# Decode attention with all of its matmuls in four column tiles, and V as the moving operand

## The chip, the core and the metric

The kernel runs on one core of a Trainium2 chip. The metric is the time of one execution in device microseconds; three runs of the kernel before gave a median of 1196.09 us (1195.54 to 1197.15). Beside them stands one profiled execution, from which all rows of the profile come.

## The reference

Two transformer layers of one decode step, for 8 sequences (batch) with one new token each. Attention and the dense block use the same weights and the same caches in both layers.

```python
# B=8, D=512, Hq=32 query heads, Hkv=8 key heads, Sk=8192 positions, Dh=128, F=1792; all bfloat16
def _A_ref(x, k_cache, v_cache, wq, wo):
    q = (x @ wq)                                  # 32 heads of 128; 4 query heads share a key head
    scores = einsum("bhqd,bhkd->bhqk", q, k) * Dh ** -0.5
    p = softmax(scores)
    o = einsum("bhqk,bhkd->bhqd", p, v)
    return o @ wo
def _B_ref(x, w1, w2):
    return silu(x @ w1) @ w2
x = x + A(layernorm(x)); x = x + B(layernorm(x))
x = x + A(layernorm(x)); x = x + B(layernorm(x))
```

For each of 8 x 8 pairs of sequence and key head, 8192 x 128 keys and as many values (2 MB each) are read and used for 4 query heads, in each of the two layers.

## The kernel before

**Tasks and loads.** A task is one layer, sequence and key head: 128 tasks. `make_tasks` orders them, so that the second layer of one sequence runs beside the first layer of later ones. A task's K comes in four granules of 512 KB, its V in four more; a granule has 16 chunks of 128 positions. The granules land in an arena of 27 slots (`NSLOT`). For 5 of the 8 key heads (20 of 32 granules of K, `KEEP`) K stays in its slots from layer 1 to layer 2, so that 40 of the 128 tasks load V alone. `plan_loads` sorts all 864 loads by the step at which they are needed and gives each a slot; `issue` (L357 to L365) writes them to SP's DMA queue, and `issue_until` sends a load as soon as the program has passed the step at which its slot's last reader stands. SP waits there (L91) for that reader's semaphore. The weights (`wq`, `wo`, `w1`, `w2`) come on the same queue near the start, and stay in SBUF.

**K's layout.** A K load puts 16 consecutive positions (4 KB) into each of 128 partitions; partition p holds positions 64 p + 16 k + c for granule k. A V load reads 512 KB that lie together: partition p holds 16 consecutive positions too, 2048 k + 16 p + c.

```python
src = cache[d.b, d.g].rearrange("(p k c) d -> k p (c d)", k=NGRAN, p=128)[d.k]   # K, L360
```

**The loop.** One loop runs over steps p of half a granule, 8 to a task. In it the instructions of all engines are written out, each engine in this order:

- `emit_q` (L463, L466): PE multiplies `pick`, a matrix of ones and zeros 128 wide, with the task's 4 query columns, four products of 128x4; DVE spreads the result into `QB`.
- `emit_t` (L444): DVE transposes K's granule in place in 32x32 blocks of 32-bit words, 1236 ns each.
- `emit_s` (L481): scores. 16 products a granule, each with 32 columns of `QB` as weights and 128 columns of K moving, in four column tiles (`t`) that write 32 partitions each of `SCp`; four tiles, four partial sums (`n`).
- softmax: `softmax_max` (L491, L493) takes each row's maximum and spreads it; `softmax_shift` (L501) adds it over partitions with an fp32 product with `ones` (128x128), DVE makes the shift (L504, L507); `softmax_exp` (L511) is the exponential on ACT, 128x512, written in permuted order into `P`; `softmax_sum` (L518, L521) adds the sums on DVE and POOL.
- `emit_pt` (L530, L534): PE transposes `P` in four products of 128x128, DVE copies them to `PT`.
- `emit_pv` (L554), `LP` = 14 steps after the scores: for each of 64 chunks, V's chunk (128x128) is the weight and 4 probability columns, each repeated `PVN` = 12 times, move past it; all 64 add up in one tile of `OTp`, 128 partitions by 48.
- `emit_norm` (L568): DVE takes every twelfth column, times the reciprocal sum (L541), as the task's output.
- between them pieces of a chain: the output projection `wo` (L652), the dense block and the next queries (L634), in products of 128x32.

A helper (`op`, `mm_group`) gives every group one semaphore; an engine runs its instructions in the order written, and waits for the readers and writers of the tiles that it touches.

Of the kernel before, what the change touches and what calls it, by code (L numbers as in the profile page):

```python
# [6 lines left out]
DH = 128  # L7
SM_SCALE = DH ** -0.5
# [4 lines left out]
GRP = 8  # L13
# [14 lines left out]
KB = 512  # L28
QUAD = 32
FAR = 1e38  # L30
PVN = 12
CW = 32
SETTLE = 2

# [174 lines left out]
def _build(ctx, nc, A_x, A_k_cache, A_v_cache, A_wq, A_wo, B_w1, B_w2, out):  # L209
# [28 lines left out]
    def sb(shape, dt, name):  # L238
        _cnt[0] += 1
        return ctx.enter_context(nc.sbuf_tensor(f"{name}_{_cnt[0]}", shape, dt))  # L240
# [30 lines left out]
    assert NGRAN == NQ and NPART * QUAD == DH  # L271
    QB = [sb([128, NPART, QUAD], BF16, "QB") for _ in range(NQB)]
    own_q = sb([128, NQ], FP32, "own_q")
    pick = sb([128, NPART, 128], BF16, "pick")
    at1 = [sb([128, HQ], BF16, "at1") for _ in range(3)]
    at2 = QT1[:, :].rearrange("p (b h) -> p h b", h=HQ)
    vr = sb([128, B], FP32, "vr")
# [10 lines left out]
    P = sb([128, KB], BF16, "P")  # L288
    Xr = P
    PT = [sb([128, CPB, NQ * USED], BF16, "PT") for _ in range(NPT)]  # L290
    ones = sb([128, 128], FP32, "ones")
    hm = sb([128, REP], FP32, "hm")
    real = sb([128, 1], FP32, "real")
    far = sb([128, NQ * USED], FP32, "far")
# [30 lines left out]
    def op(eng, inst_fn, reads=(), writes=()):  # L325
        reads = [res(n) if isinstance(n, str) else n for n in reads]
        writes = [res(n) if isinstance(n, str) else n for n in writes]
        syn.acquire(eng, reads, writes)
        inst = inst_fn()
        tok = syn.mark(inst, eng)  # L330
        syn.release(tok, reads, writes)
        return tok
# [10 lines left out]
    def mm_group(steps, reads=(), writes=()):  # L343
        def run():
            inst = None
            for f in steps:
                inst = f()
            return inst
        return op(pe, run, reads, writes)
# [7 lines left out]
    def issue(d):  # L357
        cache = A_k_cache if d.kind == "K" else A_v_cache
        if d.kind == "K":
            src = cache[d.b, d.g].rearrange("(p k c) d -> k p (c d)", k=NGRAN, p=128)[d.k]  # L360
        else:
            src = cache[d.b, d.g].rearrange("(k p c) d -> k p (c d)", k=NGRAN, p=128)[d.k]
        dst = ARENA[:, d.slot * SLOT:(d.slot + 1) * SLOT]
        dma(sp, dst, src, slsem[d.slot], writes=[r_half(d.slot, 0), r_half(d.slot, 1)])
        (k_slot if d.kind == "K" else v_slot)[(d.b, d.g, d.k)] = d.slot  # L365

    with nc.Block() as block:

        @block.sync
        def _(sync_eng):  # L370
# [12 lines left out]
            for n in range(NQB):  # L383
# [9 lines left out]
            op(dve, lambda: dve.tensor_reduce(  # L393
                own_q[:, :], ident[:, :].rearrange("p (c q) -> p c q", q=QUAD), AX.X, ALU.add),
               reads=["ident"], writes=["own_q"])
            for i in range(NPART):
                op(dve, lambda i=i: dve.tensor_copy(
                    pick[:, i, :].rearrange("p (a r) -> p a r", a=NQ),
                    ident[:, i // 2 * 2 * QUAD:(i // 2 + 1) * 2 * QUAD].rearrange("p (r e) -> p e r", e=2)[:, i % 2]
                    .unsqueeze(1).to_broadcast([128, NQ, QUAD])),  # L400
                   reads=["ident"], writes=["pick"])
            for c in range(NQ):
                op(dve, lambda c=c: dve.tensor_scalar(
                    far[:, c * USED:(c + 1) * USED].rearrange("p (r k) -> p r k", k=NGRAN),
# [48 lines left out]
            def emit_q(ti):  # L453
                layer, b, g = tasks[ti]
                if layer == 0:
                    q, rq = QT1[:, b * HQ + g * REP:b * HQ + (g + 1) * REP], f"QT1_{b}"
                else:
                    q, rq = QT2[b % 2][:, g * REP:(g + 1) * REP], f"QT2_{b % 2}"
                n = ti % NQB
                steps = []  # L460
                for i in range(NPART):
                    at = (n * NPART + i) * REP
                    steps.append(lambda i=i, at=at: pe.matmul(  # L463
                        QSp[:, at:at + REP], pick[:, i, :], q, start=True, stop=True))
                mm_group(steps, reads=["pick", rq], writes=[f"QS{n}"])
                op(dve, lambda: dve.tensor_tensor(  # L466
                    QB[n][:, :, 0:USED].rearrange("p i (r a) -> p i r a", a=NQ),
                    QSp[:, n * NPART * REP:(n + 1) * NPART * REP].rearrange("p (i r) -> p i r", r=REP).unsqueeze(3)
                    .to_broadcast([128, NPART, REP, NQ]),
                    own_q[:, :].unsqueeze(1).unsqueeze(1).to_broadcast([128, NPART, REP, NQ]), ALU.mult),  # L470
                   reads=[f"QS{n}", "own_q"], writes=[f"QB{n}"])
# [25 lines left out]

            def softmax_shift(ti):
                ob = ti % 2
                every = OTp[ob][:, 0:NQ * USED]  # L500
                mm_group([lambda: pe.matmul(every, ones[:, :], spread[:, :], start=True, stop=True)],  # L501
                         reads=["ones", "spread"], writes=[f"OT{ob}"])

                op(dve, lambda: dve.scalar_tensor_tensor(  # L504
                    own[:, :], every, real[:, 0:1], far[:, :], op0=ALU.mult, op1=ALU.add),
                   reads=[f"OT{ob}", "real", "far"], writes=["own"])
                op(dve, lambda: dve.tensor_reduce(shift[:, :], own[:, :], AX.X, ALU.min), reads=["own"], writes=["shift"])  # L507

            def softmax_exp(ti):
                bank, st = ti % NSCP, ti % NST  # L510
                op(act, lambda: act.activation(  # L511
                    P[:, :].rearrange("p (x j k) -> p k x j", x=CPB, k=NGRAN),
                    SCp[bank][:, :].rearrange("p (k x j) -> p k x j", k=NGRAN, x=CPB), ACT.Exp, bias=shift[:, 0:1], scale=SM_SCALE, accum_out=rs[st][:, :]),
                   reads=[f"SC{bank}", "shift"], writes=["P", f"rs{st}"])

            def softmax_sum(ti):
# [7 lines left out]
            def emit_pt(ti):  # L524
                pb = ti % NPT
                tb = evacs[0] % NTP
                evacs[0] += 1
                tpv = TPp[tb][:, 0:KB].rearrange("p (c q) -> p c q", q=128)
                steps = [
                    lambda c=c: pe.transpose(tpv[:, c, :], P[:, c * 128:(c + 1) * 128], ident[:, :])  # L530
                    for c in range(CPB)
                ]
                mm_group(steps, reads=["P", "ident"], writes=[f"TP{tb}"])
                op(dve, lambda: dve.tensor_copy(  # L534
                    PT[pb][:, :, :].rearrange("p x (c q) -> p x c q", q=USED),
                    tpv.rearrange("p x (c q) -> p x c q", q=QUAD)[:, :, :, 0:USED]),
                   reads=[f"TP{tb}"], writes=[f"PT{pb}"])
# [5 lines left out]
            def emit_pv(i):  # L543
                ti = i // GPT
                b, g, k, h = where(i)
                slot = v_slot[(b, g, k)]
                ob, pb = ti % 2, ti % NPT
                pv = PT[pb][:, :, :].rearrange("p x (c r k) -> p x c k r", c=NQ, k=NGRAN)
                otp = OTp[ob][:, 0:REP * PVN].rearrange("p (r n) -> p r n", n=PVN)
                steps = []  # L550
                for c in range(GRP):
                    cc = (i % GPT) * GRP + c
                    steps.append(
                        lambda c=c, cc=cc: pe.matmul(  # L554
                            otp, chunk(slot, h * GRP + c), pv[:, cc % CPB, cc // CPB % NQ, k, :].unsqueeze(2).to_broadcast([128, REP, PVN]),
                            start=(cc == 0), stop=(cc == NCH - 1),
                        )
                    )
                mm_group(steps, reads=[r_half(slot, h), f"PT{pb}"], writes=[f"OT{ob}"])

            def emit_norm(ti):
                layer, b, g = tasks[ti]
                ob, st = ti % 2, ti % NST
                if layer == 0:
                    dst, rd = at1[b % 3][:, g * REP:(g + 1) * REP], f"at1_{b % 3}"
                else:
                    dst, rd = at2[:, g * REP:(g + 1) * REP, b], f"QT1_{b}"
                op(dve, lambda: dve.tensor_tensor(dst, OTp[ob][:, 0:REP * PVN:PVN], rcp[st][:, :], ALU.mult),  # L568
                   reads=[f"OT{ob}", f"rcp{st}"], writes=[rd])

            def ln_stages(xv, rx, n):
# [198 lines left out]
            for p in range(NG + LP + GPT + 1):  # L770
# [25 lines left out]
                done = p - LP - GPT  # L796
                if done >= 0 and done % GPT == 0 and done // GPT < ntask:
                    tj = done // GPT
                    emit_norm(tj)
                    layer, b, _g = tasks[tj]  # L800
                    if layer == 0:
                        heads[b].append(_g)
                    elif b == B - 1:
                        heads[B].append(_g)
                    if layer == 0 and tj == last0[b]:
                        assert not chain and turn[0] == b
                        chain.extend([lambda b=b: add_heads(b)] * (HKV - summed[b]) + chain_of(b))
                        chain_b[0] = b
                        turn[0] = b + 1
# [49 lines left out]
```

## Time and profile before

| what | value |
|---|---|
| median of 3 runs | 1196.09 us |
| profiled execution, its own time | 1198.79 us |
| span of its profile | 1197.1 us |
| mean granted PE clock | 0.663 |
| PE / DVE / ACT / POOL busy | 839.0 / 736.1 / 183.5 / 70.8 us |
| share of 16 DMA engines' span taken by packets | 99.1% |
| bytes on SP's queue | 465.12 MB |
| loads of K / of V | 352 / 512, 512 KB each |

The page gives the span in 40 slices, with the busy share of each engine and of the DMA engines in tenths and the rate in GB/s; the queues with their packets; the chain of waits that ended last; and groups of instructions by line, with busy time, mean duration and the idle time before them. "PEld" is the load of weights on PE. A matmul's record includes its latency, so that single records overlap; the time of a group of them is better read from the timeline, which merges them.

### The profile page before, as it was taken

What the parts mean: (1) busy time and instruction counts of PE and PEld (TensorE: products, weight loads), DVE (VectorE), ACT (ScalarE), POOL (GpSimd) and SP (SyncE); (2) the same over time, 40 slices, a digit from 0 to 9 for tenths busy, and PEclk for the clock granted to TensorE, in tenths of its full rate; (3) what the DMA queues carried; (4) which work ended last, traced back from release to release, by engine and by line L of the source; (5) the groups of instructions that cost most, each with busy time, mean ns of one, the idle gap of its engine ahead of it and who ended that gap; (6) DMA issues with size and microseconds to landing.
All of it is one profiled execution on the core that took longest, in us unless ns stands there. A gap on an engine that the chain in (4) does not pass through costs nothing.

```text
span 1197.1 us, 46189 instructions
## 1 busy us (share of the span) xinstructions
PE 839.0 (70%) x20984; PEld 673.4 (56%) x20984; DVE 736.1 (61%) x1830; ACT 183.5 (15%) x266; POOL 70.8 (6%) x172
## 2 busy tenths in 40 slices
PE   1636677767776677767777778777776777677785
PEld 1435566556655566556665566556665656555564
DVE  3736763767456673867457763867376755768464
ACT  0101112111111012111111111111111111111111
POOL 0000000000000000000000000000000000000000
PEclk9955568555765577655866586756775587657765
DMA  9999999999999999999999999999999999999994
GB/s 368 385 396 397 399 355 408 407 394 395 393 408 407 368 389 401 408 404 395 389 408 408 388 397 409 407 402 395 393 407 403 399 393 408 407 392 386 402 408 165
DMA packets 131619, 468.06 MB, mean 391 GB/s; under 512 B 13904, under 2 KB 19808, under 8 KB 130912
## 3 DMA queue, kind: packets, MB, share of 16 engines
q1 hardware_dynamic: 131424, 465.12, 99.1%
q8 instruction: 164, 2.69, 0.9%
q14 instruction: 31, 0.25, 0.1%
HBM read 465.05 MB, written 0.01 MB: 388 GB/s over the span
## 4 chain that ended last, share of the span: by engine, by line
DMA 40%; PE 31%; DVE 15%; issue 9%; SPq 3%; ACT 2%; POOL 0%; POOLq 0%; ACTq 0%; DVEq 0%
DMA arena<-in_A_v_cache_dram 37%; PE OTp L554 14%; PE SCp L481 8%; DVE arena L444 7%; SPq L339 3%; DMA arena<-in_A_k_cache_dram 3%; PE MISC L634 3%; PE OTp L501 2%; PE TPp L530 2%; ACT P L511 2%; DVE rowmax L491 1%; DVE PT L534 1%; PE MISC L652 1%; DVE tr L607 1%; DVE spread L493 1%
## 5 line engine op out<-in xcount | busy, mean ns | idle before, releaser
L554 PE MATMUL OTp<-PT,arena 128*128 128x48 bf16 x8192 | 381.1, 205 | 227.6 <-DMA arena<-in_A_v_cache_dram 182.1
L444 DVE STREAM_TRANSPOSE arena<-arena 128x1024 int32<-128x1024 int32 x352 | 434.9, 1236 | 115.9 <-DMA arena<-in_A_k_cache_dram 115.2
L554 PEld LDWEIGHTS OTp<-PT,arena 128*128 128x128 bf16 x8192 | 316.9, 110 | 331.5 <-DMA arena<-in_A_v_cache_dram 242.6
L511 ACT ACTIVATE P<-SCp,shift 128x512 bf16<-128x512 f32 x128 | 180.3, 1409 | 930.6 <-DVE shift L507 651.5
L481 PE MATMUL SCp<-arena,QB 128*32 128x128 bf16 x8192 | 287.0, 275 | 37.3 <-issue 29.0
L481 PEld LDWEIGHTS SCp<-arena,QB 128*32 128x32 bf16 x8192 | 161.4, 115 | 84.1 <-issue 48.6
L521 POOL PARTITION_ALL_REDUCE ssa<-ssm x128 | 55.6, 435 | 996.0 <-DVE ssm L518 970.8
L534 DVE COPY PT<-TPp 128x256 bf16<-128x256 bf16 x128 | 37.3, 291 | 103.6 <-PE TPp L530 101.8
L501 PE MATMUL OTp<-spread,ones 128*128 128x64 f32 x256 | 75.4, 389 | 25.9 <-DVE spread L493 22.7
L491 DVE TENSOR_REDUCE rowmax<-SCp 128x1 f32<-128x512 f32 x128 | 84.8, 663 | 11.5 <-PE SCp L481 10.3
L530 PE MATMUL TPp<-ident,P 128*128 128x128 bf16 x512 | 68.8, 278 | 13.7 <-ACT P L511 9.6
L504 DVE SCALAR_TENSOR_TENSOR own<-OTp,real,far 128x64 f32<-128x64 f32 x128 | 32.9, 257 | 71.7 <-PE OTp L501 71.7
L501 PEld LDWEIGHTS OTp<-spread,ones 128*128 128x128 f32 x256 | 54.9, 266 | 35.6 <-DVE spread L493 34.4
L518 DVE TENSOR_SCALAR ssm<-hm,rs 128x4 f32<-128x4 f32 x128 | 26.8, 210 | 73.9 <-ACT P L511 73.9
L530 PEld LDWEIGHTS TPp<-ident,P 128*128 128x128 bf16 x512 | 41.7, 122 | 16.5 <-ACT P L511 12.3
L634 PE MATMUL MISC<-xnT,wq 128*128 128x32 bf16 (+1 forms) x1152 | 37.1, 185 | 19.3 <-DVE xnT L621 13.1
L634 PEld LDWEIGHTS MISC<-xnT,wq 128*128 128x128 bf16 x1152 | 35.8, 105 | 20.4 <-issue 16.3
L652 PE MATMUL MISC<-at,wo 128*128 128x32 bf16 x1024 | 37.7, 185 | 6.1 <-issue 4.4
L652 PEld LDWEIGHTS MISC<-at,wo 128*128 128x128 bf16 x1024 | 33.2, 103 | 6.9 <-issue 4.6
L463 PE MATMUL QSp<-QT,pick 128*128 128x4 bf16 x512 | 32.5, 168 | 5.7 <-DVE QT L717 2.9
L493 DVE TENSOR_SCALAR spread<-ident,rowmax 128x64 f32<-128x64 bf16 x128 | 32.6, 255 | 4.5
L511 ACT ACTIVATION_READ_ACCUMULATOR P<-SCp,shift 128x1 f32 x128 | 33.3, 260 | 0.0
(54 smaller groups left out, 276.3 us busy)
## 6 DMA issues: line engine op xcount, KB each, us to landing
arena<-in_A_v_cache_dram SPq DMA_DIRECT2D x512, 512.0 KB, 10.3
arena<-in_A_k_cache_dram SPq DMA_DIRECT2D x352, 512.0 KB, 14.5
wq<-in_A_wq_dram SPq DMA_DIRECT2D x1, 4096.0 KB, 16.6
wo<-in_A_wo_dram SPq DMA_DIRECT2D x1, 4096.0 KB, 26.3
w<-in_B_w_dram SPq DMA_DIRECT2D x2, 1792.0 KB, 22.8
P<-in_A_x_dram SPq DMA_DIRECT2D x1, 8.0 KB
out_dram<-P SPq DMA_DIRECT2D x1, 8.0 KB
```

Of the source, the lines that this page charges most:

```text
L444: op(dve, lambda: dve.transpose(words, words), reads=[r_half(slot, 0), r_half(slot, 1)], writes=[r_half(slot, 0), r_half(slot, 1)])
L481: lambda n=n, t=t: pe.matmul(SCp[bank][t * QUAD:(t + 1) * QUAD, k * 128:(k + 1) * 128], QB[qn][:, n, :], keys[:, t, n // 2, n % 2], start= ...
L491: op(dve, lambda: dve.tensor_reduce(rowmax[:, :], SCp[bank][:, :], AX.X, ALU.max), reads=[f"SC{bank}"], writes=["rowmax"])
L493: op(dve, lambda: dve.tensor_scalar(spread[:, :].rearrange("p (c q) -> p c q", q=USED), lanes, rowmax[:, 0:1], -SM_SCALE, op0=ALU.mult, op ...
L501: mm_group([lambda: pe.matmul(every, ones[:, :], spread[:, :], start=True, stop=True)], reads=["ones", "spread"], writes=[f"OT{ob}"])
L511: op(act, lambda: act.activation(P[:, :].rearrange("p (x j k) -> p k x j", x=CPB, k=NGRAN), SCp[bank][:, :].rearrange("p (k x j) -> p k x ...
L521: op(pool, lambda: pool.partition_all_reduce(ssa[st][:, :], ssm[st][:, :], 128, bass.bass_isa.ReduceOp.add), reads=[f"ssm{st}"], writes=[f ...
L530: lambda c=c: pe.transpose(tpv[:, c, :], P[:, c * 128:(c + 1) * 128], ident[:, :])
L534: op(dve, lambda: dve.tensor_copy(PT[pb][:, :, :].rearrange("p x (c q) -> p x c q", q=USED), tpv.rearrange("p x (c q) -> p x c q", q=QUAD) ...
L554: lambda c=c, cc=cc: pe.matmul(otp, chunk(slot, h * GRP + c), pv[:, cc % CPB, cc // CPB % NQ, k, :].unsqueeze(2).to_broadcast([128, REP, P ...
L634: lambda o=o, k=k: pe.matmul(MISC[:, o * n:o * n + w], w_sb[:, k, o * 128:(o + 1) * 128], rhs_of(k).to_broadcast([128, w]) if n == 1 else ...
L652: lambda o=o, h=h: pe.matmul(MISC[:, o * w:(o + 1) * w], wo_sb[:, h, o * 128:(o + 1) * 128], rhs_of(h).to_broadcast([128, w]) if n == 1 el ...
```

## The change

The change gives every attention product 32 or fewer output partitions, at one of four column tiles.

- **PV**: the 4 probability columns are the weight, and V's chunk moves (128 columns). Chunk `cc` goes to tile `cc % 4`, which writes 4 rows of 128 columns at partition 32 t of `OTp`; so each task ends with four partial sums in four partition groups.
- **fold**, new (`emit_fold`), ahead of `emit_norm`: ACT copies the 128x128 partial sums to SBUF (`OS`), and four fp32 products with `OS` as the weight and a new `pick` (128x4) moving add them up and turn them to 128 partitions by 4.
- **transposes** of `P`: 16 products of 32 columns instead of 4 of 128; exp writes `P` in order.
- **shift**: four fp32 products of 32 columns instead of one of 128.
- **queries**: 16 products with slices of `ident` as weights instead of 4 with `pick`.
- **K's source**: partition 32 a + j now holds positions 2048 a + 512 k + 16 j + c, so that the four partition groups of the scores are four blocks of positions, in the order in which V's granules are used. The runs are 4 KB as before; on the DRAM side the pattern is now 4 blocks x 32 rows x 4 KB, as the program is built, and on the arena's side 128 rows x 4 KB.

```diff
-                src = cache[d.b, d.g].rearrange("(p k c) d -> k p (c d)", k=NGRAN, p=128)[d.k]
+                src = cache[d.b, d.g].rearrange("(a k j c) d -> k a j (c d)", a=NQ, k=NGRAN, j=QUAD)[d.k]
...
-                    steps.append(lambda i=i, at=at: pe.matmul(
-                        QSp[:, at:at + REP], pick[:, i, :], q, start=True, stop=True))
+                    for a in range(NQ):
+                        steps.append(lambda a=a, at=at, pairs=pairs: pe.matmul(
+                            QSp[a * QUAD:(a + 1) * QUAD, at:at + REP], pairs, q, start=True, stop=True))
...
-                every = OTp[ob][:, 0:NQ * USED]
-                mm_group([lambda: pe.matmul(every, ones[:, :], spread[:, :], start=True, stop=True)],
+                every = OTp[ob][:, DH:DH + NQ * USED]
+                mm_group([lambda t=t: pe.matmul(every[t * QUAD:(t + 1) * QUAD, :], ones[:, :], spread[:, :], start=True, stop=True)
+                          for t in range(NQ)],
...
-                    P[:, :].rearrange("p (x j k) -> p k x j", x=CPB, k=NGRAN),
-                    SCp[bank][:, :].rearrange("p (k x j) -> p k x j", k=NGRAN, x=CPB), ACT.Exp, ...
+                    P[:, :], SCp[bank][:, :], ACT.Exp, ...
...
-                    lambda c=c: pe.transpose(tpv[:, c, :], P[:, c * 128:(c + 1) * 128], ident[:, :])
-                    for c in range(CPB)
+                    lambda c=c, k=k: pe.transpose(
+                        tpv[k * QUAD:(k + 1) * QUAD, c, :], P[:, k * 128 + c * QUAD:k * 128 + (c + 1) * QUAD], ident[:, :])
+                    for c in range(CPB) for k in range(NGRAN)
...
-                            otp, chunk(slot, h * GRP + c), pv[:, cc % CPB, cc // CPB % NQ, k, :].unsqueeze(2).to_broadcast([128, REP, PVN]),
-                            start=(cc == 0), stop=(cc == NCH - 1),
+                            OTp[ob][t * QUAD:t * QUAD + REP, 0:DH], pv[:, cc % CPB, cc // CPB % NQ, k, :], chunk(slot, h * GRP + c),
+                            start=(cc < NQ), stop=(cc >= NCH - NQ),
...
+            def emit_fold(ti):
+                ob = ti % 2
+                op(act, lambda: act.copy(OS[:, :], OTp[ob][:, 0:DH]), reads=[f"OT{ob}"], writes=["OS"])
+                folded = OTp[ob][:, DH + NQ * USED:DH + NQ * USED + REP]
+                mm_group([lambda t=t: pe.matmul(folded[t * QUAD:(t + 1) * QUAD, :], OS[:, t * QUAD:(t + 1) * QUAD], pick[:, :],
+                                                start=True, stop=True) for t in range(NQ)],
+                         reads=["OS", "pick"], writes=[f"OT{ob}"])
...
+                    emit_fold(tj)
                     emit_norm(tj)
```

At the start, the four copies that made the old `pick` give way to one reduction for the new one, and `OTp`'s first 128 columns are set to zero.

More of the change, by code (lines that the diff above doesn't have):

```diff
@@ L30 @@
 FAR = 1e38
-PVN = 12
 CW = 32
@@ L273, in _build @@
     own_q = sb([128, NQ], FP32, "own_q")
-    pick = sb([128, NPART, 128], BF16, "pick")
     at1 = [sb([128, HQ], BF16, "at1") for _ in range(3)]
@@ L290, in _build @@
     PT = [sb([128, CPB, NQ * USED], BF16, "PT") for _ in range(NPT)]
-    ones = sb([128, 128], FP32, "ones")
+    ones = sb([128, QUAD], FP32, "ones")
+    pick = sb([128, REP], FP32, "pick")
+    OS = sb([128, DH], FP32, "OS")
     hm = sb([128, REP], FP32, "hm")
@@ L395, in _ @@
                reads=["ident"], writes=["own_q"])
[L396 to L401, printed above, removed]
+            op(dve, lambda: dve.tensor_reduce(
+                pick[:, :], ident[:, :].rearrange("p (c q) -> p q c", q=QUAD)[:, 0:REP, :], AX.X, ALU.add),
+               reads=["ident"], writes=["pick"])
+            for n in range(2):
+                op(dve, lambda n=n: dve.memset(OTp[n][:, 0:DH], 0.0), writes=[f"OT{n}"])
             for c in range(NQ):
@@ L462, in emit_q @@
                     at = (n * NPART + i) * REP
-                    steps.append(lambda i=i, at=at: pe.matmul(
-                        QSp[:, at:at + REP], pick[:, i, :], q, start=True, stop=True))
-                mm_group(steps, reads=["pick", rq], writes=[f"QS{n}"])
+                    pairs = ident[:, i // 2 * 2 * QUAD:(i // 2 + 1) * 2 * QUAD].rearrange("p (r e) -> p e r", e=2)[:, i % 2]
+                    for a in range(NQ):
+                        steps.append(lambda a=a, at=at, pairs=pairs: pe.matmul(
+                            QSp[a * QUAD:(a + 1) * QUAD, at:at + REP], pairs, q, start=True, stop=True))
+                mm_group(steps, reads=["ident", rq], writes=[f"QS{n}"])
                 op(dve, lambda: dve.tensor_tensor(
@@ L511, in softmax_exp @@
                 op(act, lambda: act.activation(
-                    P[:, :].rearrange("p (x j k) -> p k x j", x=CPB, k=NGRAN),
-                    SCp[bank][:, :].rearrange("p (k x j) -> p k x j", k=NGRAN, x=CPB), ACT.Exp, bias=shift[:, 0:1], scale=SM_SCALE, accum_out=rs[st][:, :]),
+                    P[:, :], SCp[bank][:, :], ACT.Exp, bias=shift[:, 0:1], scale=SM_SCALE, accum_out=rs[st][:, :]),
                    reads=[f"SC{bank}", "shift"], writes=["P", f"rs{st}"])
@@ L548, in emit_pv @@
                 pv = PT[pb][:, :, :].rearrange("p x (c r k) -> p x c k r", c=NQ, k=NGRAN)
-                otp = OTp[ob][:, 0:REP * PVN].rearrange("p (r n) -> p r n", n=PVN)
                 steps = []
@@ L552, in emit_pv @@
                     cc = (i % GPT) * GRP + c
+                    t = cc % NQ
                     steps.append(
-                        lambda c=c, cc=cc: pe.matmul(
-                            otp, chunk(slot, h * GRP + c), pv[:, cc % CPB, cc // CPB % NQ, k, :].unsqueeze(2).to_broadcast([128, REP, PVN]),
-                            start=(cc == 0), stop=(cc == NCH - 1),
+                        lambda c=c, cc=cc, t=t: pe.matmul(
+                            OTp[ob][t * QUAD:t * QUAD + REP, 0:DH], pv[:, cc % CPB, cc // CPB % NQ, k, :], chunk(slot, h * GRP + c),
+                            start=(cc < NQ), stop=(cc >= NCH - NQ),
                         )
@@ L567, in emit_norm @@
                     dst, rd = at2[:, g * REP:(g + 1) * REP, b], f"QT1_{b}"
-                op(dve, lambda: dve.tensor_tensor(dst, OTp[ob][:, 0:REP * PVN:PVN], rcp[st][:, :], ALU.mult),
+                op(dve, lambda: dve.tensor_tensor(dst, OTp[ob][:, DH + NQ * USED:DH + NQ * USED + REP], rcp[st][:, :], ALU.mult),
                    reads=[f"OT{ob}", f"rcp{st}"], writes=[rd])
```

## The prediction

> **What bounds the kernel now.** I read the page's slices and queue counts first, then single stretches, then the waits of SP (which issues every load), and last the price of a group on PE. Rows of the page:
>
> ```profile
> DMA  9999999999999999999999999999999999999994
> GB/s 368 385 396 397 399 355 408 407 394 395 393 408 407 368 389 401 408 404 395 389 408 408 388 397 409 407 402 395 393 407 403 399 393 408 407 392 386 402 408 165
> DMA packets 131619, 468.06 MB, mean 391 GB/s; under 512 B 13904, under 2 KB 19808, under 8 KB 130912
> q1 hardware_dynamic: 131424, 465.12, 99.1%
> arena<-in_A_v_cache_dram SPq DMA_DIRECT2D x512, 512.0 KB, 10.3
> arena<-in_A_k_cache_dram SPq DMA_DIRECT2D x352, 512.0 KB, 14.5
> ```
>
> The 16 DMA engines are at work in every slice but the last, and the best slices stand at a ceiling of 408 GB/s, 25.5 GB/s for each engine. So the span is bytes: 465.12 MB / 16 = 29.07 MB per engine, 1140 us at 25.5 GB/s, of a span of 1197.1. The other 57 us: the chain of waits ends with a V transfer from 1167.01 that takes 14.94 us, so 15 us are tail; the first slice costs 3; some 39 lie in slices below 408. One of those beside a full one (columns: stretch, us, busy time of PE, PEld, DVE, ACT, POOL, PE clock, DMA share, GB/s):
>
> ```profile
> 150.00:180.00 30.00, 21.77 (x612) 18.34 (x601) 18.99 (x51) 4.25 (x6) 2.10 (x5) 0.62 0.94 355
> 360.00:390.00 30.00, 20.11 (x461) 15.79 (x458) 20.55 (x41) 4.35 (x8) 1.73 (x4) 0.56 1.03 407
> ```
>
> In the dip it is the DMA share that falls (0.94 against 1.03). What SP waits for (L91 is its semaphore wait) says why:
>
> ```profile
> SPq L91 <- PE OTp L554: 296.7, 241, 3.6
> SPq L91 <- PE SCp L481: 146.6, 146, 4.3
> ```
>
> A load is issued when PE is done with the slot's last reader; where tasks need no K (40 of 128, whose K is kept), PE frees slots too late and the queue runs dry. PE itself is busy 839 us of 1197, 6.6 us of the 9.35 us that a task lasts.
>
> **What the small packets count.** The page's packet sizes can be rebuilt from the code: a packet is one contiguous run. K and V are 864 x 128 runs of 4 KB, w1 512 of 3.5 KB (together 111104, as 130912 - 19808); wo, w2, x and out are 4096 + 1792 + 8 + 8 = 5904 runs of 1 KB (19808 - 13904). Left are 13904 packets under 512 B, which no operand accounts for. There are 870 transfers, 868 of them with 128 rows outermost and two (x and out) with 8. 868 x 16 + 2 x 8 = 13904, to the packet. So a transfer leaves one small packet for each engine that it ran on, 128 outer rows ran on 16 engines, and 8 outer rows on 8.
>
> **The change, K's loads.** This is the part that I expect to decide. Before, the source of a K load is [128 rows, 16 KB apart] x 4 KB. After, its partitions are split as (a j), and the DRAM side is [4 blocks, 512 KB apart] x [32 rows] x 4 KB; 4 and 32 can't be merged into one step. The arena's side stays 128 rows. The same 128 runs of 4 KB, in the same order into the same partitions, but the outermost count of the source is 4. If the queue cuts a transfer along its outermost count, as the 8-row ones show, only 4 equal shares can be cut on both sides: four engines take 32 rows each, the other twelve none.
>
> [...]
>
> The sum: K is 352 x 0.5243 = 184.55 MB, over four engines 46.14 MB each. Everything else, 465.12 - 184.55 = 280.57 MB, still spreads over 16: 17.54 MB each. The first four carry 63.67 MB, at 25.5 GB/s **2497 us**. The other twelve are done early, but a V load is complete only with the parts that stand behind K on the first four. A task that loads K and V takes 4 x 0.5243 / 4 / 25.5 GB/s = 20.6 us for K and 5.1 for V, 25.7 us; one with V alone 5.1.
>
> To it come the tail of 15 and the start of 3. The dips: the same 40 tasks can still starve the queue, between 0 (PE now waits for data before each such stretch, all slots are empty and the queue is full) and the 39 of today; I take 20. Sum 2535 us of span. The profiled execution took 1198.79 for a span of 1197.1 and lies 2.7 above the median of 1196.09, so these cancel within a us: **2535 us**.
>
> **The change, PE and the rest.** Prices of groups on PE (start, us, line, count) from a stretch at mostly full clock:
>
> ```profile
> 603.07 0.26 PE L463 MATMUL QSp<-QT,pick 128*128 128x4 bf16 x4
> 604.45 0.40 PE L530 MATMUL TPp<-ident,P 128*128 128x128 bf16 x4
> 606.92 0.43 PE L481 MATMUL SCp<-arena,QB 128*32 128x128 bf16 x16
> 607.27 0.57 PE L554 MATMUL OTp<-PT,arena 128*128 128x48 bf16 x16
> 607.69 0.41 PE L501 MATMUL OTp<-spread,ones 128*128 128x64 f32 x2
> ```
>
> PV takes the form of L481, which already runs as four column tiles moving 128: 0.43 instead of 0.57 for 16, four times a task, -0.56 us. The transposes become 16 of that form, 0.43 for 0.40. The query products become 16, up to 0.43 for 0.26, +0.17. The shift's fp32 product becomes four: between 0.41 (side by side) and 1.64 (in series), taken 0.6 because L481's tiles run side by side, +0.2. The fold is four more fp32 products, 0.26 to 1.64, taken 0.6. Ahead of it PE waits for ACT's copy of 128x128, between 184 ns (ACT's 128x14) and 1409 (its 128x512), some 0.5; the 16 transposes and often wo's 16 products stand between the last PV and the fold, so I count 0.2. Behind the waiting fold stand the next granule's scores, the next task's PV and with them the release of slots to SP. Net +0.6 us a task, +77 us on 839; with every upper end +2.7, some 1190 in all. At 19.8 us a task both are covered. Without that cover (K on 16 engines), 0.6 x 40 V-only tasks is 24 us, and +2.7 would fill 9.3 of 9.35 us.
>
> On DVE, the norm (L568, 132 ns) now waits for the fold, with the transposes of K (L444, 1236 ns) behind it; on ACT 128 copies of 0.5 join 184 busy us. Exp writes its 512 probabilities in order instead of permuted: between nothing and -0.75 us of its 1409 ns (L491 reads the same tile in 663); I take nothing. At the start two memsets stand for four `pick` copies (0.9 us in all). All of this lies under DMA in the forecast. PE will mostly idle, so its clock should fall from 0.66 on the mean towards the 0.50 of some windows; 839 x 0.66 / 0.50 = 1107 us still fits twice.
>
> **Rivals.**
>
> 1. *K still runs on 16 engines.* x and out have 8 rows on both sides, so their count does not say whether the source's 4 or the arena's 128 decides. If the arena's side alone does, DMA is the bound as today, 1140 + 57, and it ends not slower: PV's 0.56 us come off the V-only tasks, where PE frees slots, 40 x 0.56 = 22 at most, 1175 to 1197 and likeliest 1188. It decides from the point where slices with K loads hold over 390 GB/s. Against it: half a task's loads would need a cut of a source that has no 16 equal outer parts. If the fold is dear as well, up to 1221. Chance 0.09.
>
> 2. *Four engines that hinder each other.* K's four engines write partitions 0-31, 32-63, 64-95 and 96-127 at once, where a transfer of today gives each engine its own 8 partitions. No row shows two engines that write 32 partitions apart. At the worst each K packet takes twice as long: 46.14 MB at 12.75 GB/s is 3619, with V's 688 and the rest 38 it is 4345; at half of that hindrance 3440. It decides if K packets are stretched by more than a tenth. [...] Chance 0.14, 3000 the likeliest.
>
> [...]
>
> 3. *The forecast*, four engines at their usual rate: chance 0.77, of its own 2480 (rate 1% better, no dips) to 2645 (39 us of dips, K packets 5% longer).
>
> **How the numbers follow.** The range takes rival 3 whole and the cheaper half of rival 2, to 3000; left out are rival 1 (0.09) and the dear half of 2 (0.07). A difference of 0.2%, 2.4 us, is what runs from 1195.54 to 1197.15 can tell. Rival 1 splits into faster 0.05, same 0.02, slower 0.02; the others are all slower: 0.93.
>
> **What would show it.** In the changed profile: 352 x 12 = 4224 fewer small packets (9680 under 512 B, 127200 on q1) with the same bytes; a DMA share near 0.47 instead of 0.99 and about 183 GB/s on the mean; slices near 163 GB/s with short peaks near 400 in V-only tasks; K's time to landing doubled at least; PE's wait for V (182.1 us today at L554) above 1000 us. Wrong if the small packets stay at 13904 (rival 1), if the count falls but packets of K take over 10% longer (rival 2), or if PE or DVE, not a transfer, end the longest waits.

## The result and the profile after

| | before | after |
|---|---|---|
| median | 1196.62 us (4 runs) | 2771.58 us (2764.21 to 2795.89, 4 runs) |
| ratio | | 2.3192, 95% interval 2.3046 to 2.3338 |
| span of the profile | 1197.1 us | 2762.5 us |
| PE busy | 839.0 us | 733.6 us |

The changed kernel takes 2.3 times as long, and it is slower while PE has less to do. The page of the kernel after, its slices and its queue:

```profile
DMA  5554446444744456444654446444644446444564
GB/s 146 168 186 158 154 159 231 154 153 153 238 157 153 148 155 232 143 148 143 222 160 147 148 150 234 156 155 151 222 175 154 154 161 234 155 150 149 165 228 136
DMA packets 127435, 468.68 MB, mean 170 GB/s; under 512 B 9680, under 2 KB 15584, under 8 KB 126688
q1 hardware_dynamic: 127200, 465.10, 50.7%
```

The same bytes, but half of the DMA engines' time is empty, and the rate of most slices is 143 to 161 GB/s, with eight short peaks of 222 to 238, where the groups of five tasks without K loads stand. A slice of 69 us is longer than such a group: from 433 to 447 us the DMA share is 1.03 and the rate 410 GB/s, so V alone still runs at the full rate. Packets under 512 B have fallen from 13904 to 9680: 4224 = 352 x 12, so each K load left 4 small packets instead of 16: it ran on four engines.

PE's and DVE's groups of the page after (busy and mean, then idle time before and what ended it):

```profile
L443 DVE STREAM_TRANSPOSE arena<-arena 128x1024 int32<-128x1024 int32 x352 | 438.1, 1245 | 1631.6 <-DMA arena<-in_A_k_cache_dram 1631.6
L556 PE MATMUL OTp<-arena,PT 128*4 128x128 bf16 x8192 | 303.1, 291 | 1893.3 <-DMA arena<-in_A_v_cache_dram 1780.0
L482 PE MATMUL SCp<-arena,QB 128*32 128x128 bf16 x8192 | 308.4, 291 | 41.1 <-issue 31.8
L513 ACT ACTIVATE P<-SCp,shift 128x512 bf16<-128x512 f32 x128 | 88.0, 687 | 1869.9 <-DVE shift L509 1406.7
L565 ACT COPY OS<-OTp 128x128 f32<-128x128 f32 x128 | 34.0, 266 | 612.1 <-PE OTp L556 611.8
```

DVE waits 1631.6 us for K (115.2 before), PE 1780.0 for V (182.1 before). Little of the engines' own work is on the path: PE has 5% of the chain that ended last, DVE 1%, transfers 47% and SP's issuing of loads (L339) 43%. Two short stretches of the trace within one task show how the transfers alternate (columns as before; the last three are PE clock, DMA share, GB/s):

```profile
905.00:908.00 3.00, 0.00 (x0) 0.00 (x0) 0.00 (x0) 0.00 (x0) 0.00 (x0) 0.50 0.25 94
908.00:910.50 2.50, 0.00 (x0) 0.00 (x0) 1.91 (x3) 0.00 (x0) 0.00 (x0) 0.50 0.79 233
```

In the first only K moves: a DMA share of 0.25, four engines of sixteen, near 4 x 25.5 = 102 GB/s. In the second V moves as well, and the queue does not get back to 408: 233 GB/s over 0.79 x 16 = 12.6 busy engines is 18.4 GB/s for each, where 25.5 was the ceiling before.

### The profile page after: what moved, and what is told of

It is laid out like the page before. It is cut to its first block, busy times and chain, and to the rows that moved or that the text cites. A ratio compares the mean times of both kernels' runs of the same rounds, so it can differ in the third digit from the quotient of the medians.

```text
span 2762.5 us, 56153 instructions
## 1 busy us (share of the span) xinstructions
PE 733.6 (27%) x25848; PEld 561.8 (20%) x25848; DVE 757.5 (27%) x1829; ACT 135.9 (5%) x394; POOL 70.5 (3%) x172
## 2 busy tenths in 40 slices
DMA packets 127435, 468.68 MB, mean 170 GB/s; under 512 B 9680, under 2 KB 15584, under 8 KB 126688
## 3 DMA queue, kind: packets, MB, share of 16 engines
q1 hardware_dynamic: 127200, 465.10, 50.7%
## 4 chain that ended last, share of the span: by engine, by line
DMA 47%; SPq 43%; PE 5%; issue 4%; DVE 1%; ACT 0%; POOLq 0%; POOL 0%; DVEq 0%
DMA arena<-in_A_v_cache_dram 45%; SPq L339 43%; PE OTp L556 3%; DMA arena<-in_A_k_cache_dram 2%; PE SCp L482 1%; PE TPp L531 0%; PE OTp L567 0%; PE MISC L662 0%; PE OTp L502 0%; SPq L90 0%; DVE rowmax L492 0%; DVE arena L443 0%; PE MISC L644 0%; PE QSp L464 0%; ACT OS L565 0%
## 5 line engine op out<-in xcount | busy, mean ns | idle before, releaser
L443 DVE STREAM_TRANSPOSE arena<-arena 128x1024 int32<-128x1024 int32 x352 | 438.1, 1245 | 1631.6 <-DMA arena<-in_A_k_cache_dram 1631.6
L556 PE MATMUL OTp<-arena,PT 128*4 128x128 bf16 x8192 | 303.1, 291 | 1893.3 <-DMA arena<-in_A_v_cache_dram 1780.0
L556 PEld LDWEIGHTS OTp<-arena,PT 128*4 128x4 bf16 x8192 | 169.9, 104 | 1993.3 <-DMA arena<-in_A_v_cache_dram 1938.9
L482 PEld LDWEIGHTS SCp<-arena,QB 128*32 128x32 bf16 x8192 | 200.7, 128 | 48.6 <-issue 35.2
L513 ACT ACTIVATE P<-SCp,shift 128x512 bf16<-128x512 f32 x128 | 88.0, 687 | 1869.9 <-DVE shift L509 1406.7
L531 PE MATMUL TPp<-ident,P 128*32 128x128 bf16 x2048 | 80.1, 299 | 6.8 <-issue 3.9
L531 PEld LDWEIGHTS TPp<-ident,P 128*32 128x32 bf16 x2048 | 58.1, 140 | 8.6 <-issue 4.5
L502 PE MATMUL OTp<-spread,ones 128*32 128x64 f32 x1024 | 55.4, 304 | 16.3 <-DVE spread L494 8.4
L464 PE MATMUL QSp<-QT,ident 128*32 128x4 bf16 x2048 | 39.5, 175 | 9.9 <-issue 7.7
L464 PEld LDWEIGHTS QSp<-QT,ident 128*32 128x32 bf16 x2048 | 38.7, 119 | 11.0 <-issue 8.1
L567 PE MATMUL OTp<-pick,OS 128*32 128x4 f32 x1024 | 36.9, 201 | 6.3 <-ACT OS L565 3.1
L502 PEld LDWEIGHTS OTp<-spread,ones 128*32 128x32 f32 x1024 | 30.8, 150 | 28.3 <-DVE spread L494 18.4
```

What stands on the lines that cost most here:

```text
L443: op(dve, lambda: dve.transpose(words, words), reads=[r_half(slot, 0), r_half(slot, 1)], writes=[r_half(slot, 0), r_half(slot, 1)])
L464: steps.append(lambda a=a, at=at, pairs=pairs: pe.matmul(QSp[a * QUAD:(a + 1) * QUAD, at:at + REP], pairs, q, start=True, stop=True))
L482: lambda n=n, t=t: pe.matmul(SCp[bank][t * QUAD:(t + 1) * QUAD, k * 128:(k + 1) * 128], QB[qn][:, n, :], keys[:, t, n // 2, n % 2], start= ...
L502: mm_group([lambda t=t: pe.matmul(every[t * QUAD:(t + 1) * QUAD, :], ones[:, :], spread[:, :], start=True, stop=True) for t in range(NQ)], ...
L513: op(act, lambda: act.activation(P[:, :], SCp[bank][:, :], ACT.Exp, bias=shift[:, 0:1], scale=SM_SCALE, accum_out=rs[st][:, :]), reads=[f" ...
L531: lambda c=c, k=k: pe.transpose(tpv[k * QUAD:(k + 1) * QUAD, c, :], P[:, k * 128 + c * QUAD:k * 128 + (c + 1) * QUAD], ident[:, :])
```

## The experiments

**Which part of the change does it.** Two runs divide it: K's source alone in the kernel before, and all of the change but K's source.

```diff
# e1, in the kernel before                                  # e2: the same line the other way, in the changed kernel
-  rearrange("(p k c) d -> k p (c d)", k=NGRAN, p=128)
+  rearrange("(a k j c) d -> k a j (c d)", a=NQ, k=NGRAN, j=QUAD)
```

> The kernel before with only the new source pattern of K (4 blocks x 32 rows); the scores then belong to other positions than the V rows they are paired with. Theory (four engines): the pattern alone makes the loss, so 2720 to 2800 us, with 9680 packets under 512 B. Rival (the PE work, the fold and its waits make part of it): clearly under 2700 us.

Measured 2794.75 us (one run), beside 2764.21 to 2795.89 for the whole change, with the same count of small packets:

```profile
DMA packets 127395, 468.04 MB, mean 168 GB/s; under 512 B 9680, under 2 KB 15584, under 8 KB 126688
```

The source pattern alone makes all of the loss.

> The changed kernel with the K source of before (128 rows outermost), all else as changed; the scores then belong to other positions than the V rows they are paired with. It measures the PE part alone. Theory: DMA is the bound again, 1175 to 1221 us as the prediction's first rival has it, likeliest 1190. If PE's form gives room in the stretches without K loads: below 1190; if the fold's wait holds up the release of slots: above 1200.

Measured 1253.11 us (1252.53 to 1256.57), ratio 1.0473, interval 1.0455 to 1.0491. Sixteen engines are at work again:

```profile
q1 hardware_dynamic: 131424, 465.12, 96.2%
```

But the tiled form still costs 55 us, more than the 24 that I had worked out and outside the 1175 to 1221 of the first theory. Only "above 1200", the fold's wait, fits; the last group tests whether it is the fold.

**Does the outermost count set the engines?** The changed kernel with the four blocks cut finer.

```diff
-  a=NQ, k=NGRAN, j=QUAD
+  a=8, k=NGRAN, j=16        # e3; a=16, j=8 in e4
```

> The changed kernel with K's source cut into 8 blocks x 16 rows instead of 4 x 32; positions of K and V are paired differently. Theory (outermost count gives the engines): 8 engines, 11088 packets under 512 B; the first eight carry 184.55/8 + 17.54 = 40.6 MB, 1592 us at 25.5 GB/s; with 36 of head, tail and dips and 0.57 us lost at each of 352 pairs of a K and a V load, 1830 us (1760 to 1880). If instead each K packet is stretched by 13% (engines that hinder each other): 905 x 1.13 + 688 + 36 = 1747. If the count does not follow the blocks: 2760.

> The changed kernel with K's source cut into 16 blocks x 8 rows; positions of K and V are paired differently. Theory: 16 engines, 13904 packets under 512 B, DMA as before: 1180 to 1215 us, whatever PE's new work. Each engine now fills 8 partitions in a row, with another engine 32 partitions further: if engines that write 32 apart hinder each other by the 13% a K byte that the changed kernel would need, 452 x 0.13 = 59 us more, 1255; if they halve each other, above 1500.

Eight blocks: 2083.82 us; sixteen: 1832.68 us (one run each). Their packets:

```profile
DMA packets 128843, 468.68 MB, mean 225 GB/s; under 512 B 11088, under 2 KB 16992, under 8 KB 128096
DMA packets 131659, 468.70 MB, mean 256 GB/s; under 512 B 13904, under 2 KB 19808, under 8 KB 130912
```

The counts are those of 8 and 16 engines to the packet, so the outermost count of the source sets them. The times are not: 250 us above the forecast for eight, 580 above the old source for sixteen. The page of sixteen blocks:

```profile
GB/s 271 293 261 243 251 295 271 243 238 248 326 248 248 223 299 263 239 252 251 305 226 234 247 316 242 233 240 249 322 243 241 243 303 238 243 237 227 313 219 155
q1 hardware_dynamic: 131424, 465.12, 99.9%
```

All sixteen engines are busy for 99.9% of 1831.0 us and move the bytes that took 99.1% of 1197.1 before: 62.9 us of an engine's time per MB instead of 40.8 (share x span x 16 / MB). The packets themselves are slow. So 16 engines on K are not enough by themselves, and the second rival, engines that hinder each other, is back.

**What makes the packets slow?** If the shares follow the blocks, each engine writes 8 partitions in a row with 16 blocks, and another one at the same time the 8 that lie 32 further. The trace does not name an engine's partitions, neither here nor for the 128 rows of before. Three runs are built to keep 16 engines on K and to change which partitions are written at once. The first splits the changed kernel's load into four of 32 partitions, read from DRAM as one contiguous stretch, as V is; the other two take the old source and split it by partitions or by columns.

```diff
# f4, in the changed kernel
+  for t in range(NQ): sp.dma_start(dst[t * QUAD:(t + 1) * QUAD, :], src[t])
# h1, with the old K source
+  for t in range(2): sp.dma_start(dst[t * 64:(t + 1) * 64, :], src[t * 64:(t + 1) * 64, :])
# h2, with the old K source
+  for t in range(2): sp.dma_start(dst[:, t * 1024:(t + 1) * 1024], src[:, t * 1024:(t + 1) * 1024])
```

> The changed kernel with each K load split into four loads of 32 partitions, whose source has 32 rows outermost: the layout of the change, on 16 engines with two rows each. 13904 + 3 x 352 x 16 = 30800 packets under 512 B. If the count of engines is all: near 1200 us, up to 1260 for SP's 1056 more issues. [...]

> The changed kernel with the old K source, each K load split into two loads of 64 partitions (64 rows outermost, 16 engines each); positions of K and V are paired differently. Theory (engines that write to partitions 32 apart at once hinder each other; 16 engines on half of the partitions): packets near 250 ns, 1650 to 1900 us. Rival (16 engines are enough, the slowness of the split loads came from their number or their source): 1250 to 1310.

> As the run with partition halves, but split along the row: two loads of 128 partitions x 2 KB. The same number of loads, all partitions at once. Theory: 1250 to 1310 us (packets of 2 KB cost a little more for their bytes). If the number of loads were the cause, as slow as the partition halves.

Measured (one run each): 1851.38 us for four loads of 32 partitions, 1835.68 for halves by partitions, 1275.68 for halves by columns (22.57 above the 1253.11 of e2, the same kernel with whole loads). The pages of the last two:

```profile
DMA packets 137294, 468.74 MB, mean 256 GB/s; under 512 B 19536, under 2 KB 25440, under 8 KB 136544
q1 hardware_dynamic: 137056, 465.14, 99.9%
```

```profile
DMA packets 182350, 468.74 MB, mean 368 GB/s; under 512 B 19536, under 2 KB 25440, under 8 KB 181600
q1 hardware_dynamic: 182112, 465.14, 97.0%
```

Both have the same number of loads and of small packets, 16 engines on each, and the same source rows. The one whose K loads write half of the partitions moves 256 GB/s, the one whose K loads write all of them 368. So neither the number of loads nor the DRAM side is the cause (f4 reads contiguously and takes 1851.38 us): it is which partitions are written together. For 16 blocks, where every load writes all 128 partitions, the same cause is an inference from the equal slowness (1832.68 us). In size the loss, 1835.7 - 1275.7 = 560 us, is larger than the 452 us that K's 184.55 MB take at 408 GB/s; so K's loads by halves of the partitions moved at less than half of that rate, if V's lost nothing (an estimate from these numbers). What makes partitions written together slow, the runs do not show.

**Where the changed kernel's own excess lies.** It took 2762.5 us of span where I had 2535. My first explanation was a loss at every passage of the queue between four engines and sixteen. The test makes the passages fewer:

```diff
-  loads.sort(key=lambda d: (d.need, d.kind))
+  loads.sort(key=lambda d: (d.need // 8, d.kind))
```

> The changed kernel with the loads sorted so that four K loads come before four V loads; the queue goes between K and V 189 times instead of 687. Theory of the 236 us beyond the forecast of 2535 (lost at each passage from four engines to sixteen and back): 236 x 189 / 687 = 65 left, 2600 us (2570 to 2640). Rival (lost on each K packet, by engines that write partitions 32 apart): no change, 2740 to 2790.

Measured 2912.63 us (one run): 141 us above the changed kernel's median, where the theory had 170 less and the rival no change. The theory falls. SP's timeline of that run shows the four loads of each kind:

```profile
1523.64 9.54 SPq L339 DMA_DIRECT2D arena<-in_A_v_cache_dram  x4
1533.23 18.92 SPq L339 DMA_DIRECT2D arena<-in_A_k_cache_dram  x4
```

With the queue full, SP issues at the queue's pace: in the changed kernel, from 902.88 to 983.16 us, it issued 11 loads of K and 11 of V, 144 GB/s, and the DMA engines moved 147. In the run with K and V in fours, four K loads go in 18.92 us; the forecast's four engines need 20.6. Four V loads, 2.1 MB, go in 9.54 us, 220 GB/s where 408 would need 5.1. So it is V that is slow while K's four engines still work through theirs, not the change of kind.

The trace also holds every packet's duration, and these say the same. In the kernel before, a 4 KB packet takes 165.5 ns on the mean; in the changed kernel 195.0. Those that run while on average 3.5 to 4.6 packets are under way (34167 of 110592; only the four engines have work) take 164 ns; those with 8 to 15 under way (20759; V runs on other engines beside them) take 234. Between the first and the last 20 us, fewer than four packets are under way for only 6 us in all, so the four engines did not run dry. In the run with K and V in fours it is 97 us, so a queue that runs dry is a large part of its extra time; a later V load (its four K come first) may be why, which no run tests. That V and K collide because they write the same partitions together would fit the group above, but no run shows it for the four engines.

**What the tiled form costs on PE.** First, two versions that bring the positions together again with the old K source: exp writes in the permuted order as before, and the 16 transposes read it (f1); or exp reads in permuted order (f3).

```diff
# f1, on top of e2
-  P[:, :], SCp[bank][:, :], ACT.Exp, ...
+  P[:, :].rearrange("p (x j k) -> p k x j", x=CPB, k=NGRAN),
+  SCp[bank][:, :].rearrange("p (k x j) -> p k x j", k=NGRAN, x=CPB), ACT.Exp, ...
-  P[:, k * 128 + c * QUAD:k * 128 + (c + 1) * QUAD]      # the transposes' input
+  P[:, c * 128 + k * QUAD:c * 128 + (k + 1) * QUAD]
# f3, on top of f1: both sides "p x j k", so that the write is in order
```

> The changed kernel with the K source and the permuted exp of before, and the 16 transposes of 32 columns taken from the permuted probabilities, so that positions match again: the four-tile form with 16 DMA engines. Against the run with the old K source it adds 0.7 us of exp on each task. Theory: DMA-bound, 1175 to 1205, within 5 us of that run; faster than before only if the stretches without K loads gain from PV's shorter groups.

> As the repair with the permuted exp, but exp reads the scores in permuted order and writes the probabilities in order. If the 1409 ns of exp come from writing with a step, it falls to about 690 ns; if reading with a step costs as much, it stays near 1400. The time is that of the other repair within 3 us, since ACT is not the bound.

f1: 1259.54 us, ratio 1.0523 (1.0502 to 1.0544). f3: 1254.48 us, 1.0477 (1.0448 to 1.0506). Exp takes 1408 ns in f1 and 687 in f3: it is the write with a step that is dear, not the read. Neither beats the kernel before, and 0.7 us of exp a task moves the time by some 5 us, hardly more than the scatter of these runs (1256.17 to 1262.88 and 1248.42 to 1260.29).

What else is in the 55 us? In the trace with the old source (e2) PE stops in the middle of groups:

```profile
168.94 0.28 PE L567 MATMUL OTp<-pick,OS 128*32 128x4 f32 x4
172.60 0.20 PE L567 MATMUL OTp<-pick,OS 128*32 128x4 f32 x2 [3.38 <-issue]
```

The fold's eight products (two records for each of its four) stand ready, and after the first four 3.38 us pass before the next, and no semaphore is waited for. Such idle time, put down to issue, is the new leader of PE's waits in e2 (total, times, longest):

```profile
PE OTp L556 <- issue: 106.4, 49, 4.0
PE OTp L556 <- DMA arena<-in_A_v_cache_dram: 105.9, 88, 14.0
PE SCp L482 <- issue: 99.1, 47, 3.5
PE TPp L531 <- issue: 29.5, 13, 3.1
PE OTp L567 <- issue: 20.8, 7, 4.2
```

Against before:

```profile
PE OTp L554 <- issue: 34.6, 25, 2.8
PE SCp L481 <- issue: 29.0, 25, 2.5
```

The queue table has a row for instruction packets of 16 KB: 164 before, 202 in e2. PE's 2 x 25848 instructions (a weight load for each product) at 256 to a packet are 202; 2 x 20984 are 164. In e2 these packets start 6.1 us apart at the median and 119 of PE's 178 gaps above 1 us end 1 to 2 us after one of them has landed, where chance would give one in six. So I took the stops for waits on PE's own instructions, fetched through the busy DMA engines, and tested it with versions that hold one half of the small products each:

```diff
# f5: kernel before + new PV + fold + four shift products, 3 softmax buffers for 4 (22776 products)
# f6: kernel before + 16 query products + 16 transposes + four shift products (24824 products), old PV, no fold
```

> The kernel before with the new PV, the fold and the four shift products alone: K's source, the four query products and the four transposes are those of before (and three softmax buffers instead of four, for room). 22776 products on PE instead of 25848 (20984 before). Theory (PE stops for its next instructions: with the old K source the changed kernel lasts 1252 us for 202 instruction packets of 16 KB, 6.2 us each, and PE's idle time put down to issue rises from 75 to 287 us): 178 packets x 6.2 = 1104, under DMA's time, so 1185 to 1210 us. Rival (the fold and its wait cost the 55 us): 1235 to 1260.

> The kernel before with the 16 query products, 16 transposes and four shift products, and PV as before, without the fold. 24824 products on PE. Theory (instruction packets): 194 x 6.2 = 1203, above DMA's bare time and with little left to hide its dips, so 1205 to 1240 us. Rival (fold and PV): 1190 to 1200.

f5: 1209.09 us, ratio 1.0105 (1.0085 to 1.0124). f6: 1238.73 us, ratio 1.0355 (1.0336 to 1.0374). Their rows:

```profile
q8 instruction: 178, 2.92, 1.0%
PE SCp L487 <- issue: 58.8, 38, 2.9
PE OTp L561 <- issue: 56.0, 34, 2.8
```

```profile
q8 instruction: 194, 3.18, 1.0%
PE SCp L483 <- issue: 76.1, 47, 3.8
PE OTp L558 <- issue: 60.1, 45, 3.3
```

Both fall where the instruction theory put them, at the upper end, and the rival is out: without the fold and with the old PV the kernel loses 42.5 us, with them and few small products 12.9.

| | before | f5 | f6 | e2 |
|---|---|---|---|---|
| instruction packets | 164 | 178 | 194 | 202 |
| PE idle put down to issue, us | 79 | 151 | 174 | 299 |
| PE busy, us | 839.0 | 763.4 | 843.7 | 717.2 |
| time, us | 1196 | 1209 | 1239 | 1253 |

The time goes with the packets, not with PE's busy time. The changed kernel has the 202 packets of e2 too, but a DMA queue that is half empty, and its idle time put down to issue is 100 us instead of 299. It also gives PE more than twice the time, so this does not show by itself that the full queue is the cause. Not settled is whether each wait is the fetch itself or the queue in front of it, and no run added instructions without adding work.

## Why the prediction was right

- **K's engines** (four, with 63.67 MB each): right in their number. 9680 small packets and 127200 on the queue, as forecast to the packet; the runs with 8 and 16 blocks confirm that the outermost count sets the number (11088 and 13904 small packets), and e1 (9680) that nothing else is needed. No run shows which engines they are, so that every K load uses the same four, on which the 63.67 MB each rest, was my estimate; the runs showed a DMA share of 0.25 where only K moves, four of sixteen engines at a time.
- **The rate of those engines**: right for K alone (a share of 0.25 and 94 GB/s from 905 to 908 us, 0.28 and 109 GB/s from 912 to 914), wrong for V beside it (18.4 GB/s for each busy engine from 908 to 910.5). The term that was mis-sized is V's part of the 2497 us, the 5.1 us of V in a 25.7 us task. Slices with K loads run at about 150 GB/s instead of 163, so a task takes 4.194 MB / 150 = 28.0 us: 2.3 more, 200 us over 88 tasks, most of the 228 between 2535 and 2762.5.
- **Rival 2** had this mechanism, but in the wrong place: I priced K's engines against each other, and asked whether K packets are stretched. Where only the four engines have work they are not: a 4 KB packet takes 164 ns there, 165.5 in the kernel before. In the stretches where V runs beside K it takes 234. A K packet that takes twice as long, the term of the rival's worst end, does not show in the changed kernel: its 4 KB packets took 195.0 ns on the mean. The splits show that engines can hinder each other by the partitions they write (1835.68 against 1275.68 us). The median of 2771.58 lies above the 2480 to 2645 of the forecast's own mechanism; it is inside the stated range only because that takes in half of this rival, up to 3000. That the size lies in the range is thus partly luck; the direction and the cause are not.
- **The dips**: the 20 us were too much, since fewer than four packets were under way for only 6 us. Their upper end of 39 was what remained of 57 us; the slices below 408 add up to 29. **The share** (0.47 forecast, 0.507 measured) is higher by the longer packets.
- **PE under DMA's cover**: right that it does not matter here, wrong in both of its sizes. PE's busy time fell by 105 us where I had +77. By groups, PV lost 78 us as priced (-72); the fold took 37 where I had 77, its eight records 0.24 to 0.29 us instead of 0.6; the shift fell by 20 where I had +25. The groups' own busy times add up to only 20 us less; the other 85 us are groups that overlap more, which a sum of groups can't hold and no run takes apart. On ACT, the copy takes 266 ns instead of 0.5 us, and exp loses 0.72 of its 1.41 us. And without the cover the form costs 55 us instead of 24, most likely because I priced products by their time on PE and not by their number: the time went with the instruction packets, 1196 us with 164 to 1253 with 202.
- **Rival 1** (K still on 16 engines) is refuted by the packet counts. Its price was wrong too: the run with 16 engines and the new form is 1253 us, outside its 1175 to 1221.
- **PE's clock** fell to 0.605 on the mean from 0.663, with most slices at 0.5, as forecast. That PE's idle time lowers it is not shown: the first six slices after stand at 0.9, with PE busy for one to three tenths of them.

## What to carry to other kernels

Read a load's access pattern on both sides before its bytes: here the outermost counts said how many DMA engines run it, and the count of small packets in the profile showed it (13904 with K on sixteen engines, 11088 on eight, 9680 on four). Sixteen engines were not enough, though, when K's loads wrote halves of the partitions (1836 us, 1276 for halves by columns). The layout was dear in K's source (1575 us) and cheap in a permuted exp (0.7 us a task). Beside a full DMA queue, count a program's instructions as well as their time: with more and smaller products e2 took 1253 us instead of 1196, though its PE was busy for 717.2 us instead of 839.0.

## What was not expected of the hardware

- Sixteen engines on half of the partitions moved 256 GB/s over the whole kernel, the same loads split by columns 368.
- An ACT write of 128x512 with a step took 1408 ns, the same read with a step and written in order 687.
- PE, with nothing to wait for, stopped up to 4.2 us at a time, and the longer in all the more instruction packets its program has beside a full DMA queue: 79 us with 164 packets, 151 with 178, 174 with 194, 299 with 202 (the issue rows of PE's waits, added up).
- In the changed kernel a 4 KB packet took 164 ns while about four were under way (3.5 to 4.6 on average), 234 ns while 8 to 15 were.
